# A convolution by DFT and a soft mixture of experts on one core: the second DFT stage on sums and differences of tokens, with TensorE's order written by hand

## The chip, the cores and the metric

The kernel runs on one core of one Trainium2 chip. The core has a matrix engine (TensorE, PE in the profile; its weight loads are listed apart as PEld), a vector engine (VectorE, DVE), a scalar engine (ScalarE, ACT), a general engine (GpSimd, POOL), a queue that issues transfers (SyncE, SP), and 16 DMA engines. Matrix products are written to PSUM (eight banks of 128 x 512 f32, here four pools of two tiles each); all else lies in SBUF. The metric is device time in microseconds (us) of one execution.

## The reference

The input is `x` with 8 batches of 2496 tokens of 256 channels, f32. Each channel of each batch is convolved with a filter by an FFT over the tokens, and the 19968 resulting tokens go through a soft mixture of experts:

```python
X = np.fft.rfft(x, axis=1)
y = np.fft.irfft(X * (filt_r + 1j * filt_i)[None], n=2496, axis=1)
x = y.reshape(19968, 256)
logits = x @ phi                          # 32 slots: 8 experts of 4
d = softmax of logits over the tokens     # dispatch
slot_input = d.T @ x
slot_out[e] = relu(slot_input[e] @ w1[e]) @ w2[e]   # F = 1024
c = softmax of logits over the slots      # combine
out = c @ slot_out
```

## The kernel before, in words

2496 = 39 x 64, and the DFT is done in two stages as matrix products. The token index is split into s1 (39 values) and s2 (64 values), the frequency into t (20 values that are kept) and c (64 values). The first stage, over s1, turns 117 rows (three s2 of 39 s1) into 120 rows (three s2 of 20 t, real and imaginary). Its result goes through DRAM (`a_dram`) to put the 64 s2 with their two parts on the 128 partitions. The second stage, over s2, is one 128 x 128 matrix per t.

A batch b is worked off in these units:

- `split_x` and `s1_unit` (L299 to L324), eleven per batch from batch 1 on: ACT makes a rounded copy `xh` of 117 x 512 tokens (L305), POOL the remainder `xl` (L306), and PE adds three products in fp32r, each with 512 columns (L316). ACT copies the sum out of PSUM (L317), and a DMA writes it to `a_dram` (L321). Batch 0 uses other code (`first_unit`, `turn_ash`) and stays on the chip.
- `x_unit` (L340), ten per batch, each for two t: four f32 products, whose weights are 128 x 128 of the loaded `ash` and whose moving side is the 128 x 128 DFT matrix `b` (L347). The result, one PSUM bank `x`, is multiplied by the filter: DVE reads it twice, for `yt` and for `t2` (L360, L361), then the halves are added on DVE (L363; on POOL from batch 6 on) and subtracted on POOL (L364).
- `t_unit` (L366): four f32 transposes of 128 x 128 (L372) and a copy by ACT (L374) to `y`. After every second one eight products `l` with `phi`, 32 columns of the array each (L383).
- `chain(g)` (L396) for each of five groups of batches, (0, 1), (2, 3), (4, 5), 6 and 7, after the last unit of the group: it brings the logits to the tokens (`ltr`, `v1`, `v`, `lg`), takes the maximum (`cm`, `cmax`, `mx`, `dg`, `mb`), the exponentials (`d`), leads them back (`u`, `u2`, `dd`), sums slots (`z`, `s`, L575) and makes the row softmax for the end (`rm`, `lg`, `r_all`; L596 to L604).

After the last batch PE multiplies the experts' weights (L770 to L796), and the output stage (L816 on) writes 20.4 MB.

The program is written in a loop over 80 slots n, one `x_unit` each (L703); a scheduler then orders the instructions of every engine by its own estimates, and each engine runs its own in that order, waiting by semaphores. An f32 product is two instructions on PE, an f32 transpose or an fp32r product one.

Of the kernel before, what the change touches and what calls it, by code (L numbers as in the profile page):

```python
# [46 lines left out]
XB = 3  # L47
AB = 5
AHEAD = 5
ASH = 5  # L50
LT = 2
HOPS = 2
LATE_HOPS = 3
# [23 lines left out]

def bin_of(t, c):

    m = (c - t * pow(N1, -1, N2)) % N2  # L80
    return t + N1 * m


def shape_constants():

    s1 = np.arange(N1)
    s2 = np.array([s2_of(k) for k in range(N2)])
    w1 = np.zeros((N1, 2, NT))
# [31 lines left out]
    put("id", np.eye(P))  # L120
    put("b", bm)
# [56 lines left out]
def x_layout(x):  # L178
# [25 lines left out]
def fft_soft_moe(ctx, tc, x, fr, fi, phi, w1, w2, cst, w1q, out):  # L204
# [23 lines left out]
    m_run = [const.tile([P, SLOTS], F32, name=f"m_run{i}") for i in range(NG)]  # L228
# [26 lines left out]
    def load_x(b, c):  # L255
        if b == 0:
            t = ypool.tile([P, 2, DIM], F32, tag="y", name=f"xt0_{c}")
            sp.dma_start(t, x[0, :, 2 * c : 2 * c + 2, :])
        else:
            t = proda.tile([P, XC, DIM], F32, tag="xt", name=f"xt{b}_{c}", bufs=XB)  # L260
            i0 = c * XC
            n = min(XC, NI - i0)
            sp.dma_start(t[:, 0:n, :], x[b, :, i0 : i0 + n, :])
        xts[b, c] = t

    def first_unit(u):

        xt = xts.pop((0, u))
        pool, tag = ((ps_s1, "s1"), (ps_x, "x"))[u % 2]
        ps = pool.tile([P, 2, 2, QP], F32, tag=tag, name=f"s0_{u}")  # L270
        for i in range(2):
            for dh in range(2):
                pe.matmul(ps[:, dh, i, :], xt[0:KR, i, dh * P : (dh + 1) * P], w1q_t, start=True, stop=True)
        n = min(2 * PK, N2 - 2 * PK * u)
        to = spec[:, :, :, 4 * PK * u : 4 * PK * u + 2 * n].rearrange("d h t k -> d h k t")
        src = ps.rearrange("d h i (j r t) -> d h (i j r) t", r=2, t=NT)[:, :, 0 : 2 * n]
        if u % 2 == 1:
            dve.tensor_copy(to, src)
        else:
            act.copy(to, src)  # L280

    def turn_ash(c):
# [5 lines left out]
        ash = prod.tile([P, 2, DIM], F32, tag="ash", name=f"ash0_{c}", bufs=ASH)  # L288
# [4 lines left out]
        ashs[0, c] = ash  # L293

    a_dram = {}

    xhl = {}

    def split_x(b, u):  # L299

        c, k = divmod(2 * u, XC)
        xs = xts[b, c][0:KR, k : k + 2, :]
        xh = proda.tile([KR, 2, DIM], F32R, tag="xh", name=f"xh{b}_{u}", bufs=3)
        xl = proda.tile([KR, 2, DIM], F32R, tag="xl", name=f"xl{b}_{u}", bufs=3)
        act.copy(xh, xs)  # L305
        pool_e.tensor_tensor(out=xl, in0=xs, in1=xh.bitcast(F32), op=ALU.subtract)  # L306
        xhl[b, u] = xh, xl

    def s1_unit(b, u):
        if u == 0:  # L310
            a_dram[b] = scr.tile([N2, QR, DIM], F32, tag="a_dram", name=f"a_dram{b}")
        xh, xl = xhl.pop((b, u))
        ps = ps_s1.tile([QP, 2, DIM], F32, tag="s1", name=f"s1_{b}_{u}")
        at = proda.tile([QP, 2, DIM], F32, tag="at", name=f"at{b}_{u}", bufs=AB)
        for n, (w, xx) in enumerate(((w1h, xh), (w1l, xh), (w1h, xl))):
            pe.matmul(ps, w, xx, start=(n == 0), stop=(n == 2))  # L316
        act.copy(at, ps)  # L317
        k0 = PK * 2 * u
        dma = sp.dma_start
        if u < NH - 1:  # L320
            dma(a_dram[b][k0 : k0 + 2 * PK].rearrange("(i j) q d -> (j q) i d", j=PK), at)  # L321
        else:
            dma(a_dram[b][k0 : k0 + PK].rearrange("j q d -> (j q) d"), at[:, 0, :])
            dma(a_dram[b][k0 + PK], at[0:QR, 1, :])  # L324
# [6 lines left out]
    def load_ash(b, c):  # L331
        if b == 0:
            turn_ash(c)
            return
        t0 = 2 * c
        ash = prod.tile([P, 2, DIM], F32, tag="ash", name=f"ash{b}_{c}", bufs=ASH)
        sp.dma_start(ash, a_dram[b].rearrange("k (r t) d -> (k r) t d", t=NT)[:, t0 : t0 + 2, :])
        ashs[b, c] = ash

    def x_unit(b, c):  # L340

        t0 = 2 * c
        ash = ashs.pop((b, c))
        ps = ps_x.tile([P, 4, 2, 64], F32, tag="x", name=f"x_{b}_{c}")
        for k in range(2):
            for dh in range(2):
                pe.matmul(  # L347
                    ps[:, 2 * k + dh].rearrange("q r c -> q (r c)"),
                    ash[:, k, dh * P : (dh + 1) * P],
                    C("b"),  # L350
                    start=True,
                    stop=True,
                )
# [570 lines left out]
```

## Time and profile before

| | |
|---|---|
| three runs | 397.68, 398.8, 400.08 us; median 398.8 |
| the profiled execution | 398.73 us, of which the span is 397.0 us |
| PE busy | 367.3 us (93%) |
| DVE, ACT, POOL busy | 267.8, 215.3, 206.7 us |
| first and last `x_unit` on PE | 19.6 us, 271.8 us |
| the experts' products | 318 to 326 us |
| output stage on PE | 338 to 387 us |
| granted TensorE clock, mean | 0.95 |

A row of the groups reads: line, engine, operation, tile written <- tiles read, shape, count | busy us, mean ns of one | idle us before it, and what ended that. "128\*32" is rows by columns of the array that a product uses. A row of the timeline reads: start us, length us, engine, line, operation, tiles, shape, count. A row of the windows gives the stretch and the busy time of PE, PEld, DVE, ACT and POOL in it with their counts, the granted clock, the DMA engines' share and their GB/s.

### The profile page before, as it was taken

To read this page: it belongs to the slowest core of one execution; us is meant where nothing else is said; L and a number is where in the kernel's file an instruction comes from. 1 tells how busy PE (TensorE), PEld (TensorE's weight loads), DVE (VectorE), ACT (ScalarE), POOL (GpSimd) and SP (SyncE) were. 2 spreads that over 40 slices of the span, in tenths; PEclk is the share of its full clock that TensorE was granted. 3 is DMA by queue.
4 is the path that set the end of the run, shared out by engine and by line. 5 is a ranking of instruction groups with operands and counts; after the bars stand their busy time and mean duration, and the time that the engine had idled before them with its cause. 6 is when DMAs were issued, how large, how long until landed. Compare 5 with 4: busy or idle time off the path is not lost. (4 is left out here: it accounts for less than half of the span.)

```text
span 397.0 us, 11950 instructions
## 1 busy us (share of the span) xinstructions
PE 367.3 (93%) x4797; PEld 292.8 (74%) x4797; DVE 267.8 (67%) x465; ACT 215.3 (54%) x454; POOL 206.7 (52%) x258
## 2 busy tenths in 40 slices
PE   7998989998998999999989999999998899989980
PEld 6886778887686868887868688886766435889870
DVE  2496589874999928698996458994577222874570
ACT  2665858784667566757675343462455020654460
POOL 0499989994676666846945155662520000622200
PEclk9999999999999999999999999999999699985595
DMA  7997799997688886977886534423399993599796
GB/s 249 363 288 252 245 328 384 373 372 264 173 230 316 269 252 188 338 205 247 280 271 200 178 108 123 120 81 107 108 364 352 322 304 125 236 414 409 322 407 282
DMA packets 57481, 103.67 MB, mean 261 GB/s; under 512 B 5375, under 2 KB 34175, under 8 KB 55251
## 3 DMA queue, kind: packets, MB, share of 16 engines
q1 hardware_dynamic: 57427, 102.92, 77.1%
q8 instruction: 38, 0.62, 0.6%
q14 instruction: 16, 0.13, 0.1%
HBM read 62.78 MB, written 40.12 MB: 259 GB/s over the span
## 5 line engine op out<-in xcount | busy, mean ns | idle before, releaser
L306 POOL TENSOR_TENSOR xl<-xt,xh 117x512 fp32r<-117x512 f32 x77 | 102.0, 1332 | 17.8 <-ACT xh L305 17.3
L347 PE MATMUL x<-cst_t,ash 128*128 128x128 f32 x640 | 89.9, 281 | 3.2 <-issue 1.7
L347 PEld LDWEIGHTS x<-cst_t,ash 128*128 128x128 f32 x640 | 80.2, 191 | 12.8 <-issue 6.6
L364 POOL TENSOR_TENSOR yt<-yt,t 128x256 f32<-128x256 f32 x80 | 64.8, 812 | 39.4 <-DVE t L361 21.2
L360 DVE TENSOR_TENSOR yt<-x,fr_t 128x512 f32<-128x512 f32 x80 | 54.7, 683 | 29.7 <-PE x L347 16.4
L305 ACT CAST xh<-xt 117x512 fp32r<-117x512 f32 x77 | 47.6, 623 | 30.5 <-PE s L316 13.5
L374 ACT COPY y<-t 128x512 f32<-128x512 f32 x80 | 46.0, 590 | 29.1 <-PE t L372 27.4
L361 DVE TENSOR_TENSOR t<-x,fi_t 128x512 f32<-128x512 f32 x80 | 54.4, 680 | 2.4 <-POOL yt L364 2.2
L363 DVE TENSOR_TENSOR yt<-yt,t 128x256 f32<-128x256 f32 x60 | 51.0, 860 | 0.5
L372 PE MATMUL t<-cst_t,yt 128*128 128x128 f32 x320 | 48.5, 276 | 0.0
L317 ACT COPY at<-s 120x512 f32<-120x512 f32 x77 | 45.2, 587 | 4.6 <-PE s L316 4.1
L372 PEld LDWEIGHTS t<-cst_t,yt 128*128 128x128 f32 x320 | 37.3, 141 | 7.3 <-issue 2.7
L859 PE MATMUL out<-so_h,st 32*128 32x256 f32 x312 | 36.2, 355 | 3.1 <-ACT st L813 2.7
L316 PE MATMUL s<-xh,w1h 117*120 117x512 f32 x77 | 35.6, 462 | 2.1 <-ACT at L317 1.4
L859 PE MATMUL out<-so_l,st 32*128 32x256 f32 x312 | 34.3, 331 | 0.0
L825 POOL TENSOR_TENSOR c<-cl,r_all 117x352 f32<-117x352 f32 x8 | 6.2, 798 | 53.5 <-PE ct L839 46.8
L859 PEld LDWEIGHTS out<-so_h,st 32*128 32x128 f32 x312 | 29.8, 234 | 5.5 <-ACT st L813 3.1
L868 DVE COPY ob<-out 128x512 f32<-128x512 f32 (+1 forms) x40 | 25.4, 673 | 11.5 <-PE out L859 11.0
L316 PE MATMUL s<-xl,w1h 117*120 117x512 f32 x77 | 31.3, 407 | 0.0
L868 ACT COPY ob<-out 128x512 f32<-128x512 f32 (+1 forms) x40 | 21.5, 579 | 16.9 <-PE out L859 14.6
L316 PE MATMUL s<-xh,w1l 117*120 117x512 f32 x77 | 30.6, 397 | 0.0
L363 POOL TENSOR_TENSOR yt<-yt,t 128x256 f32<-128x256 f32 x20 | 16.2, 810 | 27.3 <-DVE t L361 15.0
(110 smaller groups left out, 566.3 us busy)
## 6 DMA issues: line engine op xcount, KB each, us to landing
xt<-in_x SPq DMA_DIRECT2D x35, 512.0 KB
ash<-a_dram SPq DMA_DIRECT2D x70, 256.0 KB
out<-ob SPq DMA_DIRECT2D x17, 1024.0 KB
a_dram<-at SPq DMA_DIRECT2D x70, 240.0 KB
w<-in_w SPq DMA_DIRECT2D x64, 256.0 KB
xt<-in_x SPq DMA_DIRECT2D x18, 256.0 KB
out<-ob SPq DMA_DIRECT2D x5, 512.0 KB
c_dram<-lg SPq DMA_DIRECT2D x2, 643.5 KB
```

The costliest lines, as they stand in the source:

```text
L305: act.copy(xh, xs)
L306: pool_e.tensor_tensor(out=xl, in0=xs, in1=xh.bitcast(F32), op=ALU.subtract)
L316: pe.matmul(ps, w, xx, start=(n == 0), stop=(n == 2))
L347: pe.matmul(ps[:, 2 * k + dh].rearrange("q r c -> q (r c)"), ash[:, k, dh * P : (dh + 1) * P], C("b"), start=True, stop=True,)
L360: dve.tensor_tensor(out=yt, in0=ps, in1=frv, op=ALU.mult)
L361: dve.tensor_tensor(out=t2, in0=ps[:, :, ::-1, :], in1=fiv, op=ALU.mult)
L363: add.tensor_tensor(out=yt[:, :, 1, :], in0=yt[:, :, 1, :], in1=t2[:, :, 1, :], op=ALU.add)
L364: pool_e.tensor_tensor(out=yt[:, :, 0, :], in0=yt[:, :, 0, :], in1=t2[:, :, 0, :], op=ALU.subtract)
L372: pe.transpose(pt[:, k, dh, :], yt[:, c % 2, 2 * k + dh].rearrange("q r c -> q (r c)"), ident)
L374: act.copy(y, pt.rearrange("k p h d -> k p (h d)"))
L859: nc.tensor.matmul(prs[k][:, mm, :], st[q, n // 2, c0 : c0 + P], (so_h, so_l)[n % 2][q, :], start=(n == 0), stop=(n == 3),)
L868: copy(ob[:, nm * k : nm * (k + 1), :], prs[k])
```

## The change

**The radix-2 step.** The 64 values of s2 are paired, s2 with s2 + 32. The sum of a pair has only the even frequencies, the difference only the odd ones. Tokens are laid out so that both of a pair stand in one load; `fold_x` makes sum and difference of 117 x 1024 values with two POOL instructions (for batch 0 the sum is on DVE). After the first stage, rows 0 to 63 of `ash` hold the sums and rows 64 to 127 the differences, and the second stage is two matrices of 64 x 64 instead of one of 128 x 128.

**The second stage and the transposes** work on 64-row halves p (or f): for each t and channel half, a product with 64 rows of weights and 64 moving columns for p = 0, then one for p = 1, to two PSUM banks. A slot now holds four t, so that there are 40 slots; a unit has 16 products and 16 transposes and fills both tiles of the pool `ps_x`, and both of `ps_t`. DVE and POOL handle halves of 128 x 8 x 2 x 32. Buffers per slot are twice as large and half as many (`ASH` 5 to 3, `YB` 34 to 19); one load of `ash` brings 512 KB instead of 256.

**The first stage** is one f32 product of 512 columns per unit in place of three in fp32r; `xh`, `xl` and the split weights are gone.

**The chain.** In `v1` and `u` two batches of a group go through one product of 64 columns of the array instead of two of 32. ACT instead of DVE copies `lsb`, `v` and `u2`. The sign flips in the filter table `fi_t` move from POOL to DVE.

**The order.** PE's order inside the slot loop is the order of the text (`manual_schedule`); the other engines are still ordered by the scheduler. The string `STEPS` says it, one entry per slot after a chain's birth: x, t and l are the units (t and l of the slot before), s a unit of the first stage, B, A, S and R pieces of the chain.

```diff
-AHEAD = 5
-ASH = 5
-LT = 2
+AHEAD = 3
+ASH = 3
+LT = 1
...
+STEPS = ("xtlss", "xtlBBsBsB", "xtAAAlss", "xtlBsBsB", "xtlBsBsB", "BxtlssB", "xtAAlss", "xtAlsBsBB", "xtlBsBsB", "xtSSSlss", "xtSSSSRlss")
...
+    def fold_x(b, c):
+
+        n = min(2, NH - 2 * c)
+        pool, tag, bufs = (x0p, "xf0", 2) if b == 0 else (proda, "xf", XF)
+        v = xts.pop((b, c))[0:KR].rearrange("s (u p) d -> s u p d", p=2)
+        xf = pool.tile([KR, 2, 2, DIM], F32, tag=tag, name=f"xf{b}_{c}", bufs=bufs)
+        step = 1 if b == 0 else n
+        for k in range(0, n, step):
+            sl = slice(k, k + step)
+            plus = dve if b == 0 else pool_e
+            plus.tensor_tensor(out=xf[:, sl, 0], in0=v[:, sl, 0], in1=v[:, sl, 1], op=ALU.add)
+            pool_e.tensor_tensor(out=xf[:, sl, 1], in0=v[:, sl, 0], in1=v[:, sl, 1], op=ALU.subtract)
...
     def s1_unit(b, u):
...
-        for n, (w, xx) in enumerate(((w1h, xh), (w1l, xh), (w1h, xl))):
-            pe.matmul(ps, w, xx, start=(n == 0), stop=(n == 2))
+        pe.matmul(ps, w1q_t, xfs.pop((b, u)), start=True, stop=True)
         act.copy(at, ps)
...
+    def x_unit(b, i):
+
+        t0 = 4 * i
+        ash = ashs.pop((b, i))
+        ps = [ps_x.tile([P, 8, 2, 32], F32, tag="x", name=f"x_{b}_{i}_{p}") for p in range(2)]
+        for k in range(4):
             for dh in range(2):
+                for p in range(2):
+                    rows = slice(64 * p, 64 * p + 64)
+                    pe.matmul(
+                        ps[p][:, 2 * k + dh].rearrange("q r c -> q (r c)"),
+                        ash[rows, k, dh * P : (dh + 1) * P],
+                        C("bx")[rows],
+                        start=True,
+                        stop=True,
+                    )
...
+        for p in range(2):
+            cs = slice(32 * p, 32 * p + 32)
...
+            dve.tensor_tensor(out=yt[:, :, :, cs], in0=ps[p], in1=frv, op=ALU.mult)
+            dve.tensor_tensor(out=t2, in0=ps[p][:, :, ::-1, :], in1=fiv, op=ALU.mult)
+            add = pool_e if b >= PA or (0) else dve
+            add.tensor_tensor(out=yt[:, :, 1, cs], in0=yt[:, :, 1, cs], in1=t2[:, :, 1, :], op=ALU.add)
+            pool_e.tensor_tensor(out=yt[:, :, 0, cs], in0=yt[:, :, 0, cs], in1=t2[:, :, 0, :], op=ALU.subtract)
+
+    def t_unit(b, i):
...
+        pts = [ps_t.tile([P, 8, 64], F32, tag="t", name=f"t_{b}_{i}_{f}") for f in range(2)]
+        for k in range(8):
+            for f in range(2):
+                rows = slice(64 * f, 64 * f + 64)
+                pe.transpose(pts[f][:, k], yt[rows, k], ident[rows, rows])
+        for f in range(2):
+            act.copy(yv[:, :, f], pts[f])
...
-                pool_e.tensor_scalar(out=sl, in0=sl, scalar1=-1.0, scalar2=None, op0=ALU.mult)
+                dve.tensor_scalar(out=sl, in0=sl, scalar1=-1.0, scalar2=None, op0=ALU.mult)
...
+    ordered.enter_context(tc.manual_schedule(engines={mybir.EngineType.PE}))
```

How the order changes is shown at three places. In names, the numbers behind `x`, `yt`, `t2`, `s1` and `xf` are batch and unit; the last number is the buffer's.

PE, a stretch of batch 1. Before:

```order
L347 MATMUL x_1_4_910<-cst_t_78,ash1_4_708 128x128 x4
L316 MATMUL s1_2_9_921<-xh2_9_857,w1h_74 120x512
L316 MATMUL s1_2_9_921<-xh2_9_857,w1l_75 120x512
L316 MATMUL s1_2_9_921<-xl2_9_858,w1h_74 120x512
L383 MATMUL l_1_0_894<-yt_1_0_763,phi_t_79 32x128 x8
```

After (each of the pairs of x and of t stands eight times):

```order
L367 MATMUL x_1_3_0_1044<-cst_t_74,ash1_3_793 128x64
L367 MATMUL x_1_3_1_1045<-cst_t_74,ash1_3_793 128x64
...
L396 MATMUL t_1_2_0_1074<-cst_t_74,yt_1_2_984 128x64
L396 MATMUL t_1_2_1_1075<-cst_t_74,yt_1_2_984 128x64
...
L409 MATMUL l_1_2_1094<-yt_1_2_984,phi_t_75 32x128 x8
L337 MATMUL s1_3_2_1104<-xf3_1_961,w1q_t_72 120x512
L337 MATMUL s1_3_3_1109<-xf3_1_961,w1q_t_72 120x512
```

Every slot now has the same sequence: a unit of x by halves, the transposes of the slot before, its `l`, then units of the first stage.

POOL, the beginning of batch 1's first stage. Before:

```order
L306 TENSOR_TENSOR xl1_2_279<-xt1_1_153,xh1_2_278 117x512
L306 TENSOR_TENSOR xl1_3_295<-xt1_1_153,xh1_3_294 117x512
L616 TENSOR_SCALAR fi_t_112<-fi_t_112 128x2x10
L616 TENSOR_SCALAR fi_t_112<-fi_t_112 128x2x22
L616 TENSOR_SCALAR fi_t_112<-fi_t_112 128x2x32 x2
L616 TENSOR_SCALAR fi_t_112<-fi_t_112 128x2x15
L616 TENSOR_SCALAR fi_t_112<-fi_t_112 128x2x17
L306 TENSOR_TENSOR xl1_4_301<-xt1_2_160,xh1_4_300 117x512
L616 TENSOR_SCALAR fi_t_112<-fi_t_112 128x2x32 x2
L364 TENSOR_TENSOR yt_0_0_310<-yt_0_0_310,t2_0_0_309 128x4x64
```

After:

```order
L294 TENSOR_TENSOR xf1_1_311<-xt1_1_144 117x2x256
L295 TENSOR_TENSOR xf1_1_311<-xt1_1_144 117x2x256
L385 TENSOR_TENSOR yt_0_0_382<-yt_0_0_382,t2_0_0_0_383 128x8x32
L385 TENSOR_TENSOR yt_0_0_382<-yt_0_0_382,t2_0_0_1_388 128x8x32
L294 TENSOR_TENSOR xf1_2_316<-xt1_2_153 117x2x256
L295 TENSOR_TENSOR xf1_2_316<-xt1_2_153 117x2x256
```

The folds of chunks 2, 3 and 4 of batch 1 now stand behind the two subtractions of the first x unit; on DVE, the two multiplications that those wait for stand behind all flips of `fi_t` (L631).

DVE, where the chain of group 0 forms the exponentials, in batch 3. Before:

```order
L494 TENSOR_TENSOR d_0_1515<-lg_0_1392,m_run0_84 117x512 x2
L494 TENSOR_TENSOR d_0_1515<-lg_0_1392,m_run0_84 117x384
L598 TENSOR_TENSOR lg_0_1392<-lg_0_1392,rm_0_1919 117x704
L360 TENSOR_TENSOR yt_3_2_1935<-x_3_2_1929,fr_t_111 128x512
L361 TENSOR_TENSOR t2_3_2_1934<-x_3_2_1929,fi_t_112 128x512
```

After:

```order
L514 TENSOR_TENSOR d_0_1778<-lg_0_1480,m_run0_80 117x512 x2
L514 TENSOR_TENSOR d_0_1778<-lg_0_1480,m_run0_80 117x384
L615 TENSOR_TENSOR lg_0_1480<-lg_0_1480,rm_0_2296 117x704 x2
L617 TENSOR_REDUCE r_all_76<-lg_0_1480 117x22 x2
L618 TENSOR_SCALAR r_all_76<-r_all_76 117x44
L619 RECIPROCAL r_all_76<-r_all_76 117x44
L381 TENSOR_TENSOR yt_3_1_1809<-x_3_1_0_1791,fr_t_104 128x16x32
```

The second subtraction and the two sums of the row softmax, which stood behind multiplications of the next units, now stand ahead of them.

More of the change, by code (lines that the diff above doesn't have):

```diff
@@ L87, in shape_constants @@
     s2 = np.array([s2_of(k) for k in range(N2)])
+    freq = np.array([freq_of(c) for c in range(N2)])
     w1 = np.zeros((N1, 2, NT))
@@ L648, in fft_soft_moe @@
             pe.matmul(pw, warm[:, 0:P], warm, start=True, stop=True)
-    tabs_next = iter(range(CPB))
+    tabs_next = iter(range(NT // 2))
     load_tables(next(tabs_next))
@@ L663, in fft_soft_moe, with start_chain @@
     late_pool = []
+    def start_chain(g):
+        gen = chain(g)
+        active.append([next(gen), gen])
     def hop(k=0):
@@ L667, in hop, with some @@
             try:
-                next(active[k][1])
+                active[k][0] = next(active[k][1])
             except StopIteration:
                 active.pop(k)
-                hop(k)
-    def hop_slot(n):
-        for _ in range(HOPS if n <= last_s1 else LATE_HOPS):
-            hop()
+    def some(kinds, n):
+        for _ in range(n):
+            k = 0
+            if len(active) > 1 and active[0][0] in "SR" and active[0][0] not in kinds:
+                k = 1
+            if k >= len(active) or active[k][0] not in kinds:
+                return
+            hop(k)
     order = [("w1", gr, fh, dh, j) for gr in range(2) for fh in range(2) for dh in range(2) for j in range(4)]
@@ L706, in fft_soft_moe @@
                 load_ash(*divmod(n + ASH, CPB))
-            if late:
-                load_tables(late.pop(0))
+            for _ in range(2):
+                if late:
+                    load_tables(late.pop(0))
             if n == CPB:
-                sp.dma_start(cst_t[:, 2 * P :], cst[:, 2 * P :])
+                sp.dma_start(cst_t[:, CS:], cst[:, CS:])
             if n == ASH:
@@ L722, in fft_soft_moe @@
             wl = iter(range(WL))
[L723 to L732 removed]
+        for _ in range(2):
+            if n > last_s1 and next(wl, None) is not None:
+                load_ws(late_pool[0], "w", 1)
+        age = n - born
+        steps = STEPS if n < NS else LATE
+        for kind in (steps[age] if 0 < age < len(steps) else steps[0]) + "s" * len(todo):
+            if kind == "x":
+                if n < NS:
+                    x_unit(*divmod(n, CPB))
+            elif kind == "s":
+                if todo:
+                    s1_unit(*todo.pop(0))
+            elif kind == "t":
+                if n >= LT:
+                    bt, ct = divmod(n - LT, CPB)
+                    t_unit(bt, ct)
+            elif kind == "l":
+                if n >= LL:
+                    bl, cl = divmod(n - LL, CPB)
+                    l_unit(bl, cl)
+                    if cl == CPB - 1 and bl in last:
+                        start_chain(last[bl])
+                        born = n
+            else:
+                some({"B": "BM", "A": "A", "S": "S", "R": "R"}[kind], 1)
+    ordered.close()
+    load_ws(ypool, "y", YB - 2 * CPB, 2)
+    load_ws(prod, "ash", ASH, 2, bufs=ASH)
     load_ws(prod, "t2", 2)
```

351 lines of the change are left out of this document (157 added, 194 removed).

## The prediction

> **What bounds the kernel now.** I read the slices first, then PE's busy time by stretch, then the groups, and last the timeline, where one sees what one instruction costs its successor.
>
> ```profile
> PE   7998989998998999999989999999998899989980
> PEclk9999999999999999999999999999999699985595
> ```
>
> ```profile
> 17.00:80.00 63.00, 59.95 (x502) 49.74 (x503) 48.51 (x67) 43.98 (x89) 61.00 (x77) 1.00 0.93 313
> 80.00:226.00 146.00, 140.85 (x1895) 112.38 (x1897) 112.37 (x181) 94.05 (x197) 92.74 (x86) 1.00 0.81 255
> 226.00:287.00 61.00, 59.96 (x997) 49.23 (x993) 45.22 (x81) 27.03 (x58) 33.31 (x45) 1.00 0.36 102
> 287.00:317.00 30.00, 25.78 (x426) 17.32 (x423) 18.08 (x58) 11.73 (x36) 2.83 (x10) 0.89 1.03 345
> 317.00:397.00 80.00, 66.36 (x896) 51.43 (x896) 37.55 (x71) 31.03 (x68) 14.53 (x36) 0.79 0.81 312
> ```
>
> From 17 to 287 us, the loop that the change rewrites, PE is busy 260.8 of 270 us at full clock and idle for 9.2; DVE is busy 206, ACT 165, POOL 187. The loop is bound by PE, and its length is the sum of what PE's instructions take, plus 9. The last chain (287 to 317) and the experts and output (80 us) hold the same work as before; I leave both alone. So the question is what PE issues per slot, a slot being four t: one new unit, two old ones.
>
> **x: no gain.**
>
> ```profile
> 120.20 0.97 PEld L347 LDWEIGHTS x<-cst_t,ash 128*128 128x128 f32 x8
> 316.98 0.52 PEld L758 LDWEIGHTS psi<-repz,s_run 128*128 128x128 f32 x4 [1.24 <-DVE s_run L585]
> L758 PEld LDWEIGHTS psi<-repz,s_run 128*128 128x128 f32 x4 | 0.5, 190 | 1.2 <-DVE s_run L585 1.2
> L480 PEld LDWEIGHTS mb<-dg,ones 32*128 32x128 f32 x10 | 1.5, 182 | 0.8 <-DVE t L361 0.4 <-issue 0.2
> 346.39 0.19 PEld L859 LDWEIGHTS out<-so_h,st 32*128 32x128 f32 x4
> 346.50 0.19 PEld L859 LDWEIGHTS out<-so_l,st 32*128 32x128 f32 x4
> 346.62 0.19 PEld L859 LDWEIGHTS out<-so_h,st 32*128 32x128 f32 x4
> ```
>
> Eight instructions of x follow each other at (0.97 - 0.19) / 7 = 0.111 us. Either the 128 columns of weights or the 128 moving columns could set this. The product psi has the same weights and 32 moving columns, and still takes (0.52 - 0.19) / 3 = 0.110; mb, with 32 rows of weights and 32 moving columns, has five pairs in 1.5 us, 0.30 each, of which 0.18 is one load: 0.12. So the load of 128 weight columns sets the step, and neither its rows nor the moving columns do. The change halves rows and moving columns, keeps the 128 weight columns and doubles the instructions, 16 to 32 per slot. What saves it is that halves can load side by side: in the output stage four loads of 32 rows stand in one row of 0.19 us, the next four 0.11 later. So 16 pairs at 0.111 = 1.78 us, as before: 0. Bounds: halves in turn, 32 x 0.111, +71 us over 40 slots; pairs at the 0.062 of the transposes below, -31.
>
> [...]
>
> **t: -15.**
>
> ```profile
> 268.58 0.91 PEld L529 LDWEIGHTS u<-cst_t,u 128*128 128x128 f32 x8
> 299.24 0.70 PEld L529 LDWEIGHTS u<-cst_t,u 64*128 64x128 f32 x10 [0.95 <-ACT u L522]
> L372 PEld LDWEIGHTS t<-cst_t,yt 128*128 128x128 f32 x320 | 37.3, 141 | 7.3 <-issue 2.7 <-ACT xh L305 0.4 <-POOL yt L364 0.2
> ```
>
> Transposes load faster, so moving columns do count: whole ones of the chain follow at (0.91 - 0.14) / 7 = 0.110, those of 64 rows at (0.70 - 0.14) / 9 = 0.062. Eight per slot at 0.110 = 0.88 become eight pairs at 0.062 = 0.50: -0.38 x 40 = -15. No row shows transposes side by side; in turn they take 0.99, +4. I take the pairs, as the output stage's row is the nearest.
>
> **First stage: +13.**
>
> ```profile
> 122.59 0.18 PEld L316 LDWEIGHTS s<-xl,w1h 117*120 117x120 f32 x1
> 122.82 0.18 PEld L316 LDWEIGHTS s<-xh,w1h 117*120 117x120 f32 x1
> 123.06 0.18 PEld L316 LDWEIGHTS s<-xh,w1l 117*120 117x120 f32 x1
> 317.93 3.64 PE L770 MATMUL h<-w,sit 128*32 128x512 f32 x32 [0.32 <-DVE sit L760]
> L770 PE MATMUL h<-w,sit 128*32 128x512 f32 x64 | 7.5, 597 | 0.3 <-DVE sit L760 0.3
> ```
>
> Three fp32r products at 0.235 make 0.70 per unit. An f32 product of 512 columns is two instructions: h runs 32 of them, four side by side, in eight rounds, (3.64 - 0.60) / 7 = 0.435 each, so 0.87 per unit. +0.17 x 77 = +13 (bounds +11 to +14).
>
> **Changes of the array's shape: +4.**
>
> ```profile
> 127.59 0.65 PE L372 MATMUL t<-cst_t,yt 128*128 128x128 f32 x4
> 128.18 0.64 PE L383 MATMUL l<-yt,phi_t 128*32 128x128 f32 x16
> 128.75 1.16 PE L347 MATMUL x<-cst_t,ash 128*128 128x128 f32 x8
> ```
>
> Four transposes are 0.44, yet `l` starts 0.59 after them; `l` is four rounds of 0.11, yet x starts 0.57 after it. Going into and out of column tiles costs some 0.14 each, in part the first load. Before there are two such changes per slot, now three (halves, `l`, whole array, halves). One more at 0.1: +4 (0 to +8).
>
> The rest of PE's work keeps its length: `v1` and `u` have half the instructions, two side by side instead of four. PE's work thus stays within +2 us of before. What decides is its waiting, now that it goes by the text.
>
> **Waiting.**
>
> ```profile
> L360 DVE TENSOR_TENSOR yt<-x,fr_t 128x512 f32<-128x512 f32 x80 | 54.7, 683 | 29.7 <-PE x L347 16.4 <-PE l L383 12.7
> L361 DVE TENSOR_TENSOR t<-x,fi_t 128x512 f32<-128x512 f32 x80 | 54.4, 680 | 2.4 <-POOL yt L364 2.2
> L363 DVE TENSOR_TENSOR yt<-yt,t 128x256 f32<-128x256 f32 x60 | 51.0, 860 | 0.5
> L494 DVE TENSOR_TENSOR d<-lg,m_run 117x512 f32<-117x512 f32 (+3 forms) x15 | 10.4, 749 | 0.1
> L598 DVE TENSOR_TENSOR lg<-lg,rm 117x704 f32<-117x704 f32 (+1 forms) x10 | 8.9, 904 | 0.0
> L601 DVE TENSOR_REDUCE r_all<-lg 117x22 f32<-117x704 f32 (+1 forms) x10 | 7.2, 729 | 0.0
> L306 POOL TENSOR_TENSOR xl<-xt,xh 117x512 fp32r<-117x512 f32 x77 | 102.0, 1332 | 17.8 <-ACT xh L305 17.3 <-PE ltr L416 0.3
> L364 POOL TENSOR_TENSOR yt<-yt,t 128x256 f32<-128x256 f32 x80 | 64.8, 812 | 39.4 <-DVE t L361 21.2 <-PE x L347 7.9 <-PE s L316 7.8
> L316 PE MATMUL s<-xh,w1h 117*120 117x512 f32 x77 | 35.6, 462 | 2.1 <-ACT at L317 1.4 <-ACT spec L280 0.5
> ```
>
> Plain slots, +2. Both tiles of x belong to one unit, so the next x waits until DVE has made four reads, 2 x 0.683 + 2 x 0.680 = 2.7 us, some 0.25 after x ends. PE has t, `l` and two first-stage units in between: 0.50 + 0.57 + 1.74 = 2.8. Short by 0.2 in nine slots without a chain (0 to +6).
>
> Chain slots, +4. In DVE's new order three `d` (2.2 us), two `lg` (1.8), two `r_all` (1.5) and two small ones stand between one unit's additions and the next unit's reads; before, reads stood after the first `lg`. From the end of x(3,0) DVE needs 2.7 + 1.7 + 5.5 = 9.9 us before the next read and 2.7 more until the bank is free; PE has about 10 us until x(3,2): t, `l`, two units, `mb`, x, t, `u`, `l`, three units. So x(3,2) is late by nearly 3 us, and behind it on PE everything is. At the maximum (`mt` behind `cmax`) PE also waits for three reductions, some 2 us. That is 5 per group, 15 for three; I take 10, since the second group's reads stand earlier. The loop already idles 5.1 + 1.0 = 6 us from 80 to 287, which I count as these same waits: net +4 (-6 to +9).
>
> First slot, +4. Ten units of batch 1 stand together behind x(0,0). POOL needs 2 x 1.33 = 2.7 us per fold of two units, PE 1.74. Three folds, 8.0 us, stand behind two subtractions that wait for DVE's reads, and these for all the flips: 2.7 + 0.8 + 8.0 = 11.5 us in which PE has 8.7. With some 4 us for the tables to land, less the 3 that PE idles there now: +4 (0 to +9).
>
> Saved, -2: a unit no longer queues behind ACT's rounded copies (the 2.1 us before L316). That ACT loses L305 otherwise frees an engine that nobody waits for. POOL's folds, 70 at 1.33 and 14 shorter, replace 102 us of `xl`; the flips move to a DVE with room in the first stretch; DMA bytes are the same: 0 each.
>
> Sum: 0 - 15 + 13 + 4 + 2 + 4 + 4 - 2 = +10 on a span of 397.0, that is 407; with the 1.7 us around it, 409 (the profiled 398.73 is the median).
>
> **Rivals.** *Faster*: the text's order closes the gaps. For it: DVE, ACT and POOL have 60 us and more to spare over the loop. Then no new wait comes and the 9.2 go: -15 + 13 + 4 - 2 - 9 = -9, 390. It decides if PE's idle time before x for DVE stays under 2 us in all and slot 0 under 13. Chance 0.18. *x really shortens*: pairs go at 0.062, -31; then PE has 1.2 us of cover less and DVE's reads hold it oftener, giving back about a third: 409 - 21 = 388. Against it: psi. 0.06. *No change*, 397 to 401: half of the new waits, +5, less the 6 counted above. 0.13. *Halves do not overlap*: +71 for x and +19 for t against the sum, 499. Against it the output stage. 0.05. *Forecast*, 401 to 422: 0.58.
>
> **Numbers.** Within 0.5% of 398.8 a measurement of this kernel can't tell from no change. Faster 0.18 + 0.06 = 0.24; same 0.13; slower 0.58 + 0.05 = 0.63. The range 390 to 424 leaves out half of the faster rival's spread, some of the shorter x, and the case of halves in turn; the forecast's own range is 401 to 420.
>
> **What would show it.** Right: loads of x two by two, 0.11 us from pair to pair, transposes at 0.06; first-stage instructions 0.43 apart; idle before x ended by DVE's `t2` (L382), longest in batches 3 and 5; a first slot of over 15 us. Wrong: x at 0.06 per pair, or a PE idle for less than 9 us in the loop (too slow); single loads of x, or transposes at 0.06 in turn (too fast).

## The result: 10% slower, and the profile after

The changed kernel took 438.47 us in the median of 4 runs (433.59 to 438.92), the kernel before 398.24 beside it: a ratio of 1.098, 95% interval 1.089 to 1.108. The forecast was 409, slower, and the range ended at 424. So the sign was right and the size was not: +10 forecast, +40 measured. The profiled execution took 438.41 us with a span of 436.5.

The two rows of slices of the changed kernel, TensorE's busy tenths and its granted clock:

```profile
PE   7696999999988999998979999788997979999980
PEclk9988999999987899999699999955999799995795
```

Before, the clock row read 9 from the first slice to the end of the loop. Now it dips inside the loop, five times, and the last dip fills two slices. The busy time by stretch (columns: stretch, its length, busy us and instructions of PE, PEld, DVE, ACT and POOL, granted clock, DMA share, GB/s), first of the changed kernel, cut at the first x, the last x, psi and the first output:

```profile
28.00:311.90 283.90, 261.83 (x3458) 183.49 (x3457) 169.37 (x296) 133.41 (x281) 165.70 (x174) 0.92 0.67 207
311.90:358.10 46.20, 39.99 (x703) 30.82 (x702) 18.37 (x56) 22.89 (x61) 9.09 (x19) 0.93 0.75 252
358.10:378.90 20.80, 20.02 (x227) 9.33 (x227) 4.48 (x9) 3.41 (x7) 1.12 (x2) 1.00 0.75 205
378.90:436.50 57.60, 43.22 (x673) 38.63 (x673) 32.92 (x64) 27.33 (x61) 13.41 (x35) 0.79 0.87 357
```

and of the kernel before, cut at the same events:

```profile
19.50:269.70 250.20, 241.17 (x3108) 197.16 (x3107) 197.76 (x312) 155.63 (x323) 177.04 (x189) 1.00 0.76 243
269.70:317.00 47.30, 42.86 (x690) 29.52 (x689) 25.72 (x73) 18.83 (x50) 10.35 (x20) 0.93 0.76 253
337.80:397.00 59.20, 46.34 (x673) 42.10 (x673) 33.06 (x63) 27.63 (x61) 13.40 (x35) 0.72 0.85 347
```

The first x starts at 28.0 us in place of 19.5: +8.5. From the first to the last x it takes 283.9 in place of 250.2: +33.7. From the last x to the end it takes 124.6 in place of 127.3: -2.7. Together +39.5, the whole difference of the spans. So everything is lost up to the last x, and most of it inside the loop.

What the instructions themselves do there is what was forecast. One plain slot of the changed kernel on TensorE:

```profile
62.61 0.67 PE L396 MATMUL t<-cst_t,yt 64*128 64x64 f32 x16
63.20 0.65 PE L409 MATMUL l<-yt,phi_t 128*32 128x128 f32 x16
63.78 1.98 PE L337 MATMUL s<-xf,w1q_t 117*120 117x512 f32 x4
65.69 1.55 PE L367 MATMUL x<-cst_t,ash 64*128 64x64 f32 x24
```

t takes 0.59 us to the start of `l`, `l` 0.58, four first-stage instructions 1.91. The weight loads show the steps themselves:

```profile
62.50 0.64 PEld L396 LDWEIGHTS t<-cst_t,yt 64*128 64x128 f32 x16
65.68 1.42 PEld L367 LDWEIGHTS x<-cst_t,ash 64*128 64x128 f32 x24 [0.77 <-PE s L337]
```

One load of x lasts 0.19 us, so twelve pairs of x follow each other at (1.42 - 0.19) / 11 = 0.112 us; one load of t lasts 0.14, so eight pairs of t follow at (0.64 - 0.14) / 7 = 0.07. But the same instructions look otherwise at other places. Two stretches of the windows and the timeline from 127 us on:

```profile
128.70:135.50 6.80, 6.80 (x51) 3.69 (x49) 3.68 (x6) 1.85 (x4) 1.56 (x2) 0.50 0.45 147
282.30:306.00 23.70, 20.21 (x247) 18.43 (x247) 14.94 (x28) 8.26 (x18) 9.22 (x12) 0.50 0.22 68
```

```profile
127.22 0.26 PE L493 MATMUL mt<-cst_t,cmax 117*32 117x117 f32 x1 [1.84 <-DVE cmax L489]
...
129.74 1.07 PE L396 MATMUL t<-cst_t,yt 64*128 64x64 f32 x16
130.74 1.08 PE L409 MATMUL l<-yt,phi_t 128*32 128x128 f32 x16
131.75 3.77 PE L337 MATMUL s<-xf,w1q_t 117*120 117x512 f32 x4
...
142.56 1.08 PE L409 MATMUL l<-yt,phi_t 128*32 128x128 f32 x16 [2.25 <-ACT u L540]
```

After a wait of 1.84 us for `cmax` the granted clock is 0.50 for 6.8 us, and the same t and `l` take 1.7 times their time, the first stage 1.9 times. Five such stretches lie between the first and the last x: 3.4 us at 36.5, 6.8 at 128.7, 3.4 at 142, 6.8 at 207, 23.7 at 282. TensorE is busy in them for 40.4 us. I count half of that as lost: 20.2 us. This is an upper figure, since t and `l` do not take quite twice as long; by their 1.7 throughout it would be 16.6. The rest of the loop follows: TensorE idles 283.9 - 261.8 = 22.1 us in place of 9.0, so +13.0; and the work at full clock is 261.8 - 20.2 = 241.6 us against 241.2, so +0.4 (up to +4.0 with the lower figure). The sum of the whole: 8.5 + 20.2 + 13.0 + 0.4 - 2.7 = 39.4.

The waits of TensorE in the changed kernel, from 17 to 320 us (columns: who waits for whom, us in total, times, longest):

```profile
PE mt L493 <- DVE cmax L489: 4.8, 3, 1.8
PE l L409 <- ACT u L540: 4.6, 2, 2.4
PE s L337 <- POOL xf L295: 3.8, 2, 2.9
PE x L367 <- issue: 2.9, 1, 2.9
PE ash L321 <- DVE spec L314: 2.5, 1, 2.5
PE ltr L439 <- ACT lsb L440: 2.0, 3, 0.7
```

### The profile page after: what moved, and what is told of

Its sections match the earlier page's. It is cut to its first block, busy times and chain, and to the rows that moved or that the text cites. A ratio compares the mean times of both kernels' runs of the same rounds, so it can differ in the third digit from the quotient of the medians.

```text
span 436.5 us, 12472 instructions
## 1 busy us (share of the span) xinstructions
PE 385.9 (88%) x5176; PEld 279.9 (64%) x5176; DVE 245.6 (56%) x486; ACT 196.4 (45%) x424; POOL 203.8 (47%) x247
## 5 line engine op out<-in xcount | busy, mean ns | idle before, releaser
L367 PEld LDWEIGHTS x<-cst_t,ash 64*128 64x128 f32 x1280 | 82.0, 201 | 23.7 <-issue 14.6
L367 PE MATMUL x<-cst_t,ash 64*128 64x64 f32 x1280 | 88.0, 289 | 4.0 <-issue 2.9
L385 POOL TENSOR_TENSOR yt<-yt,t 128x256 f32<-128x256 f32 x80 | 62.3, 781 | 60.9 <-DVE t L382 60.4
L337 PE MATMUL s<-xf,w1q_t 117*120 117x512 f32 x154 | 81.8, 645 | 3.8 <-POOL xf L295 3.8
L294 POOL TENSOR_TENSOR xf<-xt 117x512 f32<-117x512 f32 (+1 forms) x42 | 51.5, 1226 | 30.6 <-issue 25.5
L295 POOL TENSOR_TENSOR xf<-xt 117x512 f32<-117x512 f32 (+1 forms) x53 | 59.7, 1132 | 5.6 <-DMA xt<-in_x 4.6
L337 PEld LDWEIGHTS s<-xf,w1q_t 117*120 117x120 f32 x154 | 26.6, 196 | 33.0 <-issue 23.1
L384 DVE TENSOR_TENSOR yt<-yt,t 128x256 f32<-128x256 f32 x60 | 39.4, 695 | 0.0
L907 PE MATMUL out<-so_h,st 32*128 32x256 f32 x312 | 33.7, 329 | 3.2 <-ACT st L861 2.7
L409 PE MATMUL l<-yt,phi_t 128*32 128x128 f32 x640 | 27.9, 296 | 5.8 <-ACT u L540 4.6
L384 POOL TENSOR_TENSOR yt<-yt,t 128x256 f32<-128x256 f32 x20 | 15.0, 751 | 36.3 <-DVE t L382 36.3
L907 PEld LDWEIGHTS out<-so_h,st 32*128 32x128 f32 x312 | 27.2, 210 | 6.0 <-ACT st L861 3.0
L396 PE MATMUL t<-cst_t,yt 64*128 64x64 f32 x640 | 29.5, 234 | 0.8 <-POOL yt L385 0.8
L396 PEld LDWEIGHTS t<-cst_t,yt 64*128 64x128 f32 x640 | 28.5, 156 | 1.2 <-POOL yt L385 1.2
```

What stands on the lines that cost most here:

```text
L294: plus.tensor_tensor(out=xf[:, sl, 0], in0=v[:, sl, 0], in1=v[:, sl, 1], op=ALU.add)
L295: pool_e.tensor_tensor(out=xf[:, sl, 1], in0=v[:, sl, 0], in1=v[:, sl, 1], op=ALU.subtract)
L337: pe.matmul(ps, w1q_t, xfs.pop((b, u)), start=True, stop=True)
L367: pe.matmul(ps[p][:, 2 * k + dh].rearrange("q r c -> q (r c)"), ash[rows, k, dh * P : (dh + 1) * P], C("bx")[rows], start=True, stop=True,)
L384: add.tensor_tensor(out=yt[:, :, 1, cs], in0=yt[:, :, 1, cs], in1=t2[:, :, 1, :], op=ALU.add)
L385: pool_e.tensor_tensor(out=yt[:, :, 0, cs], in0=yt[:, :, 0, cs], in1=t2[:, :, 0, :], op=ALU.subtract)
```

## The experiments

The theory at this point: TensorE's work is as long as before; short waits cost twice, once themselves and once in a halved clock after them. The rivals: the waits alone, with the clock a by-product; or work on 64-row halves that is longer than the sum says.

**The order left to the scheduler.** One line goes:

```diff
-    ordered.enter_context(tc.manual_schedule(engines={mybir.EngineType.PE}))
```

> One edit: the loop's TensorE order is left to the scheduler again; arithmetic, tiles and the other engines' text stay. Theory (waits and the half clock they bring cost the missed 30 us; TensorE's work is as long as before): idle of TensorE in the loop falls from 25 us to under 12, the granted clock stays at 1.00 between unit 1 and the last x, the late first slots stay; 405 to 415 us. Rival (the new work on 64-row halves is itself longer than the sum says): still over 430 us with little idle time.

It took 461 to 472 us, so even its shortest time is 22 us over the changed kernel's; the profile is of one of 472. The idle time goes as expected, but what is then left is far longer. Its windows, its group of x and one of its rows of x:

```profile
25.60:343.50 317.90, 316.72 (x3461) 233.59 (x3460) 178.33 (x315) 132.57 (x277) 165.90 (x171) 0.92 0.62 185
300.00:337.50 37.50, 37.50 (x284) 30.91 (x285) 20.17 (x35) 11.32 (x23) 10.14 (x14) 0.50 0.18 57
...
L367 PE MATMUL x<-cst_t,ash 64*128 64x64 f32 x1280 | 145.0, 289 | 0.1
...
78.36 2.00 PE L367 MATMUL x<-cst_t,ash 64*128 64x64 f32 x18
```

TensorE idles 1.2 us and is busy 316.7. x is busy 145.0 us where the changed kernel has 88.0 (each with its stretches at half clock; ahead of those at the end, an instruction of x takes 0.106 us on average here and 0.065 there). In the row shown, 18 instructions of x take 2.00 us, where the changed kernel has 24 in 1.55: most halves no longer run side by side. That the scheduler parts them is read from these steps; the trace does not name the half. It is the case "halves do not overlap", which I held at 0.05; the order by hand is what keeps it off. By the numbers the rival was met (over 430 us with little idle time), but the run can't decide, since it changed two things at once: waits and pairs. It shows one thing more: from 300 us on TensorE is busy without a gap for 37.5 us, and the clock stays at 0.50.

**Idle products in the waits.** Products that nobody reads stand where TensorE waits for `cmax` and for ACT's copies of u: first five per place, then two.

```diff
-"BxtlssB", "xtAAlss",
+"FBxtlssB", "xtAAFlss",
+                if kind == "F":
+                    pf = ps_s1.tile([P, 512], F32, tag="s1", name=f"fill_{n}_{age}")
+                    for _ in range(5):                     # then range(2)
+                        pe.matmul(pf, C("id"), cst_t[:, 0:512], start=True, stop=True)
```

> TensorE gets five 512-column products that nobody reads ahead of mt (which waits there 1.5 to 1.8 us for cmax) and five behind the first two u pieces (where the next l waits 2.3 us): the waits last as long as before, but TensorE is busy in them. Theory (a stretch with too little TensorE work halves the granted clock, and that costs as much again): the half-clock stretches at 128, 142, 207 and 282 us go, 47 us of half clock in the loop become under 15; 416 to 424 us. Rival (the waits alone cost the time, the clock is a by-product): 436 to 442 us.

443.22 us (ratio to before 1.115, 1.107 to 1.123): not as the theory had it, and just over the rival's 436 to 442. The half-clock stretches at 128, 142 and 207 us went, yet from the first to the last x it took 286.4 us. I had taken 0.43 us for a product that consists of two instructions of 0.43: the five lasted 4.4 us in waits of 1.8 and 2.3 and gave back what the clock gained (the slots from 115.6 to 145.6 us took 30.0 us, in the changed kernel those from 117.5 to 147.4 took 29.9). So the same was run with two.

> As the run with five idle products, but two of them: an f32 product of 512 columns takes two instructions of 0.43 us, so two last 1.7 us, inside the waits of 1.9 and 2.3 us, where five lasted 4.3 and outlasted them. From the first x to the last x the changed kernel takes 283.9 us. Theory (the clock, apart from the waits): the waits stay as they are, the half-clock stretches at 128, 142, 207 go and the 24 us at 282 shrink: 268 to 274 us. Rival (the clock costs nothing, TensorE waits for others anyway): 282 to 286 us.

430.82 us (1.084, 1.076 to 1.091). From the first to the last x 276.0 in place of 283.9, 2 us over the expected range. The stretches at 128, 142 and 207 are gone, the last one shrank from 23.7 to 13.6 us. The lost clock, counted as before, fell from 20.2 to 6.3 us, the products add 10.9 of busy time, and the idle time is 4.9 shorter (17.2): 283.9 - 13.9 + 10.9 - 4.9 = 276.0. So the clock is worth some 13.9 us here, about half of it eaten by what the products outlast. The rival, 282 to 286, falls. It was not yet the whole of it.

**The waits taken out by order.** The x of one slot goes ahead of `mt`, and `l` and first-stage units between the pieces of u:

```diff
-"BxtlssB", "xtAAlss", "xtAlsBsBB"
+"xBtlssB", "xtlAsAs", "xtAlsBsBB"
```

> Only the table of steps is changed: the x of that slot goes ahead of mt, so that it runs while DVE forms cmax, and the l and two first-stage units go between the two u pieces that stood together. Theory (a wait of 2 us costs itself and then a stretch at half clock): 10 us of waits and some 15 to 20 of lost clock go: 405 to 416 us. Rival (waits alone): 427 to 431 us. Second rival (something else becomes late at once, as everything behind TensorE is tight): over 433 us.

425.11 us (1.072, 1.060 to 1.083), between theory and rival: 271.1 us from the first to the last x. The stretches at 128, 142 and 207 went, but 17.1 us of the last one stayed, with TensorE busy for most of it:

```profile
275.00:292.10 17.10, 14.21 (x176) 13.29 (x178) 11.21 (x21) 6.12 (x13) 6.54 (x10) 0.50 0.20 62
```

With the 37.5 us without a gap above, a busy TensorE does not by itself bring the clock back. Which work does was measured next.

**The clock by itself.** Behind the last output of the changed kernel stands a measurement; its results are not used. Each form of the kernel's work runs alone, first after a gap of some 7 us, then from full clock:

```diff
+    for f, n in ((full, 55), (xhalf, 228), (xwhole, 216), (thalf, 420), (twhole, 218), (lcol, 218), (ucol, 240), (orow, 200)):
+        gap(14); run_for(f, n); run_for(full, 32); run_for(f, n); run_for(full, 16)
+    for n in (1, 2, 3, 4, 5, 6):
+        run_for(full, 32); gap(n)
```

> The changed kernel with a measurement behind its last output, whose results nobody reads: for each form of TensorE work a gap, then about 24 us of that form alone, then 14 us of full 512-column products, the form again at full clock, and full products; at the end gaps of growing length between full products. Theory (what the clock follows is how full the array is, not whether TensorE has an instruction): after the gap x on halves, transposes on halves and the 32-column l stay at clock 0.50 for all of their 24 us, full products return to 1.00 within 7 us; started at full clock, the same forms fall to 0.50 too or stay, which would tell one threshold from two. Rival (any busy TensorE counts): every form returns to 1.00 within 7 us and none falls.

The windows of that run: x on halves after the gap, the same from full clock, whole x until the clock rises and from there on, then the transposes on halves and `l` until it rises:

```profile
577.80:675.00 97.20, 97.19 (x912) 97.19 (x912) 0.00 (x0) 0.62 (x1) 0.00 (x0) 0.50 0.00 1
705.50:756.40 50.90, 50.90 (x913) 50.90 (x912) 0.00 (x0) 0.00 (x0) 0.00 (x0) 1.00 0.01 2
777.10:782.60 5.50, 5.46 (x25) 5.46 (x26) 0.00 (x0) 0.62 (x1) 0.00 (x0) 0.50 0.01 3
782.80:828.10 45.30, 45.30 (x408) 45.30 (x407) 0.00 (x0) 0.00 (x0) 0.00 (x0) 1.00 0.00 1
...
924.40:929.80 5.40, 5.40 (x104) 5.40 (x106) 0.00 (x0) 0.62 (x1) 0.00 (x0) 0.52 0.02 3
...
1125.20:1131.00 5.80, 5.79 (x112) 5.37 (x116) 0.00 (x0) 0.62 (x1) 0.00 (x0) 0.50 0.01 3
```

x on halves stayed at 0.50 for all of its 97 us, with TensorE busy throughout. Seven other forms, `l` and the transposes among them, were back at 1.00 after 3.4 to 5.8 us: there the theory was wrong. Started at full clock, x on halves kept 1.00 for all of its 51 us: it kept the clock that it did not bring back. Both forms of x cost the same at full clock: 456 pairs on halves in 50.9 us are 0.112 each, 408 whole ones in 45.3 are 0.111. In the loop it is the same: halves go at 0.112 per pair, and a plain slot takes 4.91 us with halves and, in the next run, with whole x.

**x whole again, and nothing else.** The two halves become one block-diagonal matrix of constants, a tile of x per two t:

```diff
-    put("bx", bx)
+    bw = np.zeros((2, N2, 2, 2, half))
+    for p in range(2):
+        bw[p, :, :, p] = bx.reshape(2, N2, 2, half)[p]
+    put("bx", bw.reshape(P, P))
...
-                    pe.matmul(ps[p][:, 2 * k + dh]..., ash[rows, k, dh * P : (dh + 1) * P], C("bx")[rows], ...)
+                    pe.matmul(ps[:, 2 * k + dh]..., ash[:, 2 * h + k, dh * P : (dh + 1) * P], C("bx"), ...)
```

> The changed kernel with x undone alone: again on all 128 rows with 128 moving columns (the two halves as one block-diagonal matrix of constants), a tile of x per two t. First x to last x is 283.9 us in the changed kernel. Theory (at full clock x takes the same 1.78 us per slot either way, but only whole x brings a halved clock back): the 24 us at half clock at 282 us become 7 or less and the stretches of 7 us become 3.4; with DVE's reads starting one half earlier some 2 us of waits go too: 268 to 276 us. Rival 1 (x on halves is cheaper at full clock): over 286 us. Rival 2 (no difference): 282 to 286 us with the same half-clock stretches.

413.37 us (1.039, 1.031 to 1.046): 25 us less than the changed kernel, from one edit that changes next to nothing in TensorE's work at full clock. Its loop is shorter than the theory's 268 to 276 us:

```profile
27.40:286.80 259.40, 244.35 (x2835) 175.11 (x2834) 178.76 (x300) 132.36 (x281) 170.49 (x176) 0.99 0.72 227
```

Of the 24.5 us between 283.9 and 259.4, the lost clock, counted as before, is 18.8 (one stretch of 3.4 us, 1.4 lost, is left of 20.2) and the idle time 7.0 (15.1 in place of 22.1; DVE can now read the first tile while the second is made, and the waits of `l` for ACT's copies of u fell from 4.6 to 0.5, but which of the two did how much was not tried); the work is 1.3 longer. This is the largest single cause.

**Gaps between bursts.** What was still open: why waits of 1.5 us halved the clock in the changed kernel, and 1.7 us did not twice with whole x. Again behind the last output: plain slots without a first stage after a gap, and bursts with short gaps.

```diff
+    for f in (mixhalf, mixwhole):          # x (halves or whole), t on halves, l
+        gap(14); run_for(f, 8); run_for(full, 32)
+    for f, n in ((xhalf, 24), (xwhole, 23), (thalf, 88), (full, 11)):
+        run_for(full, 16)
+        for _ in range(8):
+            run_for(f, n); gap(3)
```

> The changed kernel with a second measurement behind its last output. First, after a gap, eight plain slots without a first stage (x, transposes on halves, l), with x on halves and with x whole. Theory: with x on halves the clock stays at 0.50 for longer than two 3.4 us windows or for all eight slots, with whole x it is back at 1.00 within 7 us. Rival: both are back within 7 us. Then, for x on halves, whole x, transposes on halves and full products, at full clock eight times 5 us of the form and a gap of some 1.7 us. Theory (a form that fills the array less lets a shorter gap halve the clock): x on halves falls to 0.50, whole x and full products do not, or in fewer of the eight. Rival (the gap alone decides): all forms alike.

The windows: eight slots with x on halves, eight with whole x, then the bursts of x on halves, whole x, transposes on halves, full products; and from the timeline one burst of x on halves and one of whole x, each with its gap:

```profile
433.50:477.00 43.50, 43.50 (x512) 39.51 (x512) 0.00 (x0) 0.56 (x1) 0.00 (x0) 0.50 0.01 2
512.90:540.30 27.40, 27.40 (x380) 24.41 (x384) 0.00 (x0) 0.62 (x1) 0.00 (x0) 0.92 0.01 2
589.00:673.00 84.00, 73.48 (x672) 72.17 (x672) 8.84 (x21) 4.32 (x7) 0.00 (x0) 0.50 0.00 1
696.00:742.80 46.80, 37.58 (x322) 36.44 (x322) 7.77 (x19) 4.33 (x7) 0.00 (x0) 1.00 0.00 1
765.60:814.40 48.80, 39.60 (x1230) 38.78 (x1232) 7.71 (x19) 4.34 (x7) 0.00 (x0) 1.00 0.01 3
841.00:917.50 76.50, 67.32 (x153) 28.68 (x154) 7.72 (x19) 4.32 (x7) 0.00 (x0) 1.00 0.00 0
```

```profile
601.02 10.50 PE L953 MATMUL mic<-mw 64*128 64x64 f32 x96 [1.52 <-DVE mw L989]
...
703.05 5.40 PE L953 MATMUL mic<-mw 128*128 128x128 f32 x46 [1.51 <-DVE mw L989]
```

As the theory had it, in both parts. Slots with x on halves do not leave 0.50 in 43.5 us, with whole x the clock is back 4.6 us after the start. The same gap of 1.5 us takes the clock behind the first burst of x on halves, after which it does not come back, and not once behind eight bursts of each of the other forms (the bursts of full products were 9.7 us long). Where the gap lies against the steps of 3.41 us in which the clock changes is not the reason: it ends 0.1 us before such a step with x on halves, and the last three of the eight gaps of whole x lie wholly between two steps, as it does. That explains the 23.7 us at the loop's end, where the first stage has run out and x, t and `l` are most of what is left.

**Terms of the sum.** On the version with whole x the transposes are made whole too:

```diff
-                pe.transpose(pts[f][:, k], yt[rows, k], ident[rows, rows])
+                pe.transpose(pts[f][:, k], yt[:, 4 * f + k], ident)
```

> On the version with whole x (413.4 us): the transposes are whole again too, 8 per slot in place of 8 pairs of halves. The prediction's term for the halves is -15 us (0.88 to 0.50 per slot), and one change of the array's shape more per slot costs +4. Theory (both terms are right and TensorE bounds the loop): 8 plain slots at 5.2 us in place of 4.9, the first x to the last x 259.4 becomes 268 to 273, 422 to 427 us. Rival (transposes are hidden, since others bound the loop): 411 to 415 us.

421.98 us; from the first to the last x 266.3 in place of 259.4, so +6.9, just under the theory's ranges and far from the rival's. Plain slots take 5.14 us in place of 4.91. The term is real and TensorE bounds the loop, but it is 0.23 per slot, 9 us, where the sum had 0.38 less 0.1, 11.

The first stage as three fp32r products again (on the repaired version below, with one x buffer and two `at` fewer for room):

```diff
-        pe.matmul(ps, w1q_t, xfs.pop((b, u)), start=True, stop=True)
+        for n, (w, xx) in enumerate(((w1h, xh), (w1l, xh), (w1h, xl))):
+            pe.matmul(ps, w, xx, start=(n == 0), stop=(n == 2))
```

> On the version with whole x, the moved mt and the new start (404.4 us): the first stage of batches 1 to 7 as three fp32r products again, of the folded rows rounded by ACT and the remainder by DVE. It has two x buffers in place of three and three at in place of five, for room. Theory (the term +13 of the sum: 0.70 in place of 0.87 us per unit on the engine that bounds the loop): -10 to -13, 391 to 395 us, which would be faster than the kernel before. Rival (the rounded copies and POOL's and DVE's longer queue hold the units, which is what the change removed): 403 to 412 us.

426.49 us, the rival, and worse than it. Slots with pieces of the chain and two units that don't wait fall from 7.5 to 7.2 us, 0.15 per unit as the term has it (0.17). But units now wait for the remainders on DVE:

```profile
PE s L352 <- DVE xl L309: 8.2, 7, 2.3
PE l L423 <- ACT u L554: 5.2, 2, 3.3
```

The waits more than eat the term, also through the clock (five stretches in the loop). How much of it the missing buffers did was not tried.

**The start.** Two edits on the version with the changed table of steps (425.1 us): the sums of batch 1's folds on DVE, and the flips on POOL again.

```diff
-            plus = dve if b == 0 else pool_e
+            plus = dve if b <= 1 else pool_e
```

> On the version with the changed table of steps (425.1 us): the sums of batch 1's folds go from POOL to DVE, which stands idle for 13 us of the first slot. Theory (the first slot waits for POOL's folds, 2.6 us per two units against 1.74 on TensorE): from the first x to the second x 17.7 us become 11 to 13.5, the whole 418 to 421 us. Rival (the first slot is held by the loads or the tables): 17 us and 424 to 426 us.

428.71 us, no gain: 17.5 us from first to second x. With both engines at it, POOL's two differences took 4.28 us (2.1 each, against 1.26), and DVE then waited 4.8 us for one of the two fold buffers.

```diff
-                dve.tensor_scalar(out=sl, in0=sl, scalar1=-1.0, ...)
+                pool_e.tensor_scalar(out=sl, in0=sl, scalar1=-1.0, ...)
```

> On the same version: the flips of the tables go back from DVE to POOL. Theory (the first x is late because DVE's flips stand ahead of the copies that the first stage of batch 0 waits for): the first x starts at 22 to 25 us in place of 27.7, the half clock at 22 us goes; what POOL gets costs nothing there, as it stands idle from 20 to 31 us; 420 to 423 us. Rival (POOL then folds later and the first slot takes the gain back): the second x stays at 45 us, 424 to 428 us.

427.07 us. The first x came at 23.3 in place of 27.7, as expected, and the second at 44.6, as the rival said: POOL's next folds stand behind the flips and begin at 32.8 (33.7 without the edit).

**Repairs put together.** On whole x: first the x of one slot ahead of `mt`, then also four first-stage units ahead of batch 0's transposes and the flips on ACT, then also a product nobody reads ahead of each block of outputs.

```diff
-"BxtlssB", "xtAAlss"
+"xBtlssB", "xtAAlss"
```

> On the version with whole x: the x of one slot per group goes ahead of mt, which waits 1.7 us for cmax three times. Theory: three waits of 1.7 us and the last half-clock stretch (3.4 us) go, 259.4 us from first to last x become 252 to 255, 405 to 409 us. Rival (mb and the d behind it become late by as much): no change, 411 to 415 us.

410.64 us (1.037, 1.028 to 1.046); 256.4 us from first to last x. Some half of the expected gain: `mt` still waits 0.95 us (1.7 before), and 1.2 us then stand ahead of one `mb`.

```diff
-                dve.tensor_scalar(out=sl, in0=sl, scalar1=-1.0, ...)
+                act.mul(sl, sl, -1.0)
...
+    fold_next(0)
+    for _ in range(4):
+        s1_unit(*at_slot[0].pop(0))
     for c in range(ASH):
         load_ash(0, c)
-    fold_next(0)
```

> As that, and the start: four first-stage units of batch 1, whose folds are done by 20 us, stand ahead of the transposes of batch 0, where TensorE waits 3.6 us for DVE, and the flips go to ACT, which has 9 us free from 12 to 27. Theory (DVE's flips delay the first x, and TensorE's 10 units of one slot wait for POOL because their first two buffers are given back late): first x at 24 to 27 us, second x 9 to 11 later in place of 14.9; 396 to 402 us. Rival (the loads hold the start): 404 to 409 us.

404.37 us (1.020, 1.012 to 1.029), over the 396 to 402 expected and at the rival's number. The second x comes 9.3 us after the first in place of 14.9, as expected, but the first, at 27.2, hardly moved (27.5). The clock is 1.00 throughout the loop:

```profile
27.20:278.80 251.60, 238.92 (x2828) 172.87 (x2827) 170.43 (x284) 130.50 (x282) 164.02 (x173) 1.00 0.74 234
```

```diff
+        if nm == 2:
+            nc.tensor.matmul(prs[0]..., ident, cst_t[:, 0:512], start=True, stop=True)
```

> As that, and in the output stage one f32 product of 512 columns that nobody reads ahead of each block of outputs, 19 of them, 0.87 us each. The output stage took 41.3 us where the clock stayed at 1.00, 46.3 with 13.7 us at half clock, 48.8 in the kernel before with 24. Theory (waits for ACT's st in that stage halve the clock, and 32-row products do not keep it): the stage stays at 1.00 and takes 41 to 44 us where it had a half-clock stretch, gain 0 to 5 us. Rival (the added 16 us of TensorE work outlast the waits): the stage takes over 50 us and the kernel is slower than without by 3 to 10 us.

413.48 us, the rival: from the first output to the end 67.1 us in place of 57.7. No version beat the kernel before. The nearest takes nearly as long as it from the first to the last x (251.6 against 250.2, with four first-stage units, 3.5 us, moved ahead of the first x); what is left is the first x, 27.2 against 19.5 us.

## Why the prediction was wrong, step by step

**Work of TensorE: right.** The sum was 0 - 15 + 13 + 4 = +2; the loop at full clock grew by 0.4, by the lower count of lost clock 4. x goes by pairs at 0.112 (0.111 forecast), transposes by pairs at 0.07 in the slot shown and 0.063 alone (0.062), first-stage instructions 0.43 apart. t and the changes of shape together came out as -9 with -11 forecast, so a change of shape costs nearer 0.15 than 0.1 per slot; the first stage came out as 0.15 per unit for 0.17.

**The step that failed: "x: no gain", 0.** I costed halves by how long they take at full clock, and there 0 was right. The step had no term for what they do to the clock, and the sum ran through a loop "at full clock" as if that were a property of the loop. Undoing this edit alone gave back 25 us of the 40: some 18.8 of clock, and 7.0 of waits. (The +2 that I gave the plain slots for DVE's reads did not come either: they take 4.9 us without a wait.)

**Waiting, +8: too little.** The loop's idle time grew by 13.0. The chain's 15 gross was near: `mt` behind `cmax` 4.8 (6 forecast), x behind DVE's rows 3.5 in one place (9 forecast, in three), and 4.6 that I did not see, `l` behind ACT's copies of u. What failed was the netting: I took 10 for 15 and set the kernel's old 6 us against them. And of the three waits for `cmax` (1.8, 1.5 and 1.5 us) and the two long ones for u (2.25 and 2.4), all but the last then cost a stretch at half clock. The wait of 2.4 us, from 220.1 to 222.5 us, did not; a step of the clock's grid (see the last section) falls inside it, at 220.8, but no run shows whether that is the reason.

**First slot, +4: the mechanism right, the place too late.** POOL's folds did stand behind two subtractions that waited for DVE (17.7 us in the slot, "over 15"), and by the sixth x the loop was 4.7 behind its own start. The flips had no part in that wait: DVE idled 1.1 us for x itself before its first read. But the first x was itself 8.5 late. "The flips move to a DVE with room in the first stretch: 0" was the wrong step: with the flips back on POOL the first x came 4.4 earlier, though the second did not gain from it. The rest lies in the folds and copies ahead of it and was not taken apart.

**Rivals.** "Faster" and "no change" fell with the first slot and the idle time. "x really shortens" is out: pairs at 0.112. "Halves do not overlap" is what most slots show with the scheduler's order, not with the order by hand.

**The signs.** Loads two by two, transposes at 0.06 to 0.07, 0.43 and a first slot over 15 us showed as listed. "Idle before x ended by DVE, longest in batches 3 and 5" did not: those batches waited before `mt` and `l`, and x waited in batch 7.

## What to carry to other kernels

Cost an edit twice: by its time at full clock, and by how much it makes the array do per time, since a form can, like x on halves here, take the same time with half the work (0.112 us a pair, 0.111 a whole one) and then neither keep the clock over a short wait (0.50 behind a gap of 1.5 us) nor bring it back (97 us at 0.50). A wait on the engine that sets the end can cost more than itself (6.8 us at 0.50 behind one of 1.84): look at the granted clock behind it, stretch by stretch. Where tiles must go in pairs, the order has to keep them adjacent; in the scheduler's order x was busy for 145 us in place of 88.

## What the runs showed of the hardware that was not expected

- The stretches at half clock last 3.4, 6.8, 13.6, 17.1 or 23.9 us, multiples of 3.4, and in the changed kernel their starts lie on one grid (22.9, 36.5, 128.7, 142.3, 207.2 and 282.3 us are whole steps of 3.41 apart). In its loop waits of 1.5 to 2.9 us were enough to halve the clock (one of 2.4 us was not), and behind its last output 97 us of a TensorE without a gap did not bring it back when the work was x on halves.
- What sets x on halves apart would fit the columns streamed per time: 64 per pair of 0.112 us, 0.57 per ns, where whole x has 128 in 0.111 (1.15) and transposes on halves 64 in 0.063 (1.0). That is a reading of these forms; no run varied the columns alone.
- Transposes, too, bring the clock back: alone after a gap, both forms were back at 1.00, whole ones in 4.6 us and halves in 5.2.
- Between full products gaps of 0.6, 1.05 and 1.5 us left the clock at 1.00, gaps of 2.0 and 2.4 us halved it.
- In the output stage half clock costs little: 57.7 us from first output to end in the nearest version, with all products at 1.00, 59.2 with 24 us at half in the kernel before, and behind the last product there still follow 16 us (from 385.9 to 402.1 us) of copies and transfers.
